# Relu-squared attention and a GELU layer pair: one more batch of the first layer as seven half-size products, in a new order of operations

## The chip, the cores and the metric

The kernel runs on one core of a Trainium2 chip. The metric is the device time of one run, in microseconds (us), given as the median of some runs. The engines have the short names of the profile: PE is TensorE (matrix products), PEld its weight loads, DVE is VectorE, ACT is ScalarE, POOL is GpSimd, SP is SyncE. A "q" behind a name (SPq, POOLq) is the engine's own queue of instructions, among them the issues of DMA transfers.

## The reference

Attention with relu squared in place of softmax goes straight into a two-layer perceptron with exact GELU. There are 8 batches, 12 heads, 448 positions and head size 64; the perceptron sees 3584 rows of 768 columns and has 2048 hidden columns. Inputs and output are float32.

```python
scores = (q @ k.transpose(0, 1, 3, 2)) / sqrt(64)       # 8 x 12 x 448 x 448
attn = maximum(scores, 0) ** 2 / 448
attn_out = attn @ v                                     # 8 x 12 x 448 x 64
x = attn_out.transpose(0, 2, 1, 3).reshape(3584, 768)
h = x @ w_in                                            # 3584 x 2048
g = 0.5 * h * (1 + erf(h / sqrt(2)))
out = g @ w_out                                         # 3584 x 768
```

## The kernel before

**Attention.** The work goes by batch (0 to 7) and, in a batch, by three groups of four heads. One step (`add_steps`) makes the scores of one 128-row block of K for all 448 columns of Q: two products each into the two halves of a PSUM tile `ps`, on quarters of PE's array (64 x 64, L736). ACT or DVE then takes relu into `a_sq` (L748, L750), and DVE squares it in place (L757). After seven steps of a group `add_av` multiplies by V (L797, also 64 x 64) into `pav`, and two copies put the result into `xT`, the transposed input of the perceptron. `QK2.1` below means the scores of batch 2, group 1.

**Where Q and K come from.** POOL issues the loads of Q, K, V and of both weight matrices, which also turn float32 into bf16. Q and K must be transposed. Batches 0 and 1 do so on PE (`add_tk`, `add_tq`). Batches 2 to 7 use DMA transposes issued by SP (`add_T_dma`, L662): nine for each batch, three per group, which are K, the even slots of Q and the odd slots of Q. The odd slots of a group also need the Q load of the next group. POOL keeps its loads apart from transposes by gates: `add_gate(b, g)` (L703) is a small copy of what group g's transposes have written, so that POOL, and all that it has to issue after that, waits until these have landed. `qT` and `kT`, the tiles that transposes write, exist twice, and so the transposes of batch b wait for the scores of batch b - 2.

**The first layer** reads `xT` of a batch. In the plain form (`add_f1`, L849) it is 16 column blocks of six products with 448 moving columns, with the result in `psh`; ACT applies GELU into `h_sb` (L859). In block form (`add_blocks`, `add_block`, L993) the layer is cut as a 2 x 2 block matrix (halves of the 768 inputs, of the 448 rows, and of the 2048 outputs), and a scheme with seven half-size products in place of eight is used. Its sums of weights (`add_wsums`) are made once on DVE; for each batch DVE also makes four sums of x halves (`xsum`, tile `xs`), and combines the products in passes (`passed`, L1030, tile `part`), from which ACT takes GELU (L1039). Before the change batches 5, 6 and 7 have this form; their weight sums overwrite part of `w_in`, so the last plain first layer must be over.

**The second layer** runs over 14 groups of 256 rows (`add_group`), each again by seven products (L1166) of 8 x 384 columns. DVE makes sums of `h_sb` (L1147) and combines the products into two tiles `osb` of 128 rows (L1200), which SP stores (`store_rows`, L1127). There are three `osb` buffers; each group takes two, and a buffer is free when its store has landed. The last product of the last group is cut in two, of `LAST` and 384 - `LAST` columns. The rows of group 0 are done plainly (`add_plain`).

**The order.** All of these are operations given to a `Scheduler`, which numbers them as they are added. The order in which each engine issues its operations is written out in a string, `ORDER`. A word is an engine (P for PE, A for ACT, D for DVE, G for POOL, S for SP) and an operation's number; `Z` and a number stands for a filler on PE (`add_fill`), products with zeros of so many columns, that are used for nothing. Every engine issues strictly in the order of its words; an operation that is not ready holds all behind it on its engine. What waits on what follows from the data and the tile buffers.

Of the kernel before, what the change touches and what calls it, by code (L numbers as in the profile page):

```python
# [26 lines left out]
KF = FF // 128  # L27
# [24 lines left out]
LEAD = 8  # L52
HALF_M = 6
# [30 lines left out]
G0 G1 G2 G3 G1435 G4 G5 G6 A10 P11 D13 A16 P17 G7 D12 P14 D18 P42 P39 G8 P19 A15 P21 D43 P33 P36 D44  # L84
A40 D20 Z128 A22 P54 G9 P25 P23 A37 D34 P51 D26 P48 A55 Z1056 D35 A24 P69 D56 Z1024 D41 A49
P57 Z992 D38 A52 P63 Z448 G117 D70 P45 A58 D53 P66 A64 D50 P27 A46 G118 P31 D59 P60 D28 A67
G119 D32 A47 P78 P29 D65 G120 A61 P81 Z1088 D68 D30 A79 P93 D62 P108 Z544 D71 A82 P84 Z992
G121 A94 P75 D109 P72 G122 D83 A85 P90 P129 D80 G123 D73 A76 P105 A74 P102 D95 G124 P131 D130
A91 P141 D86 A106 D77 P111 P96 D132 A103 P165 P143 D92 A112 D104 D107 A97 P156 D113 P87 G125
D98 A166 P99 D110 G126 D88 A157 P114 A142 D100 A89 P174 G127 A101 P168 D115 P133 A144 P135  # L90
A116 G128 D175 P171 P159 A169 D134 P251 D136 D170 A160 P145 D158 A172 D167 A252 P162 P186 D176
P192 P243 A146 D161 G147 D173 A187 G148 P253 D193 A163 A244 D164 P195 G149 P180 P198 P137 A254
G150 P139 D196 A181 P183 P177 G151 D138 A199 D140 A184 P189 P219 P245 D178 G152 A190 D185 P247
G153 D194 A220 D179 A246 G154 P213 D188 P222 P204 P263 D221 A248 G155 D197 A214 D200 P265 D191
A205 D182 A264 P261 A223 A266 P216 D224 S231 P207 P201 D206 A262 A208 S229 P210 P259 D209 A217
D215 S232 P255 D211 A260 P249 D212 D218 A256 D202 P225 A203 S228 A250 P257 S230 A226 P267 D227
A258 P348 S234 A268 P350 S233 A349 P352 G237 A351 G238 P354 S235 A353 G239 P288 S236 P294 P282
P358 A355 G240 G241 D289 P356 D283 A359 P360 D295 A357 D290 P306 P279 P276 D296 P362 A361 D307
P364 D280 A363 P366 D277 A365 P368 A367 P370 A369 P300 P285 P291 G242 P372 A371 G269 D286 A292
P374 G270 D284 A373 G271 P318 P303 D301 P312 G272 P376 D308 A375 G273 A304 D319 P378 D278 A377  # L100
P380 D313 A379 D293 G274 D314 D390 P382 D305 G275 D302 A381 D391 D287 D281 P330 P309 P297 S398
D392 A331 D320 P315 S399 P384 D393 A298 D396 A310 S401 A383 D417 P387 D394 D419 A385 D311 A299
D395 A316 D317 P324 P321 D418 A325 P333 D397 P327 A388 P421 D420 D322 S400 A328 D323 P423 D326
A334 D422 S386 P339 P336 P342 P425 D424 D329 A343 D335 P427 S402 A426 D337 P429 G407 A340 G408
S403 D428 P431 G409 D344 D338 S389 D341 P440 P437 D332 P345 S404 D430 A438 P443 D441 P446 S405
P433 D432 A346 D347 A444 P509 A447 D434 P511 D439 G410 D448 S406 A510 G411 P449 D442 P452 G412
P455 P513 D562 A512 S435 D445 S436 A453 P515 D454 A450 A514 P517 D456 D451 P464 D457 P461 P458
S541 A465 P467 D462 A518 P470 G413 S542 P519 A516 G414 A459 G415 P521 D471 S543 G416 D472 A520
P523 D466 A468 D460 S544 A522 P479 D560 P476 P473 D469 P525 A524 D463 A477 P527 D480 A474 D478
A526 P529 D475 D481 A528 P488 P485 P482 S545 A489 P494 D486 A530 P491 P531 D487 D483 P533 D495  # L110
A532 S546 P535 D496 A484 D561 A492 P503 D490 P500 A534 P497 D493 P537 A536 G550 G551 S547 P564
D498 G552 A538 D504 S548 P539 D499 A501 G553 A565 D505 P600 G554 D502 P603 P506 G555 S549 A601
P606 D604 A540 P609 P566 D563 A507 D602 P568 D607 D567 P570 D610 A569 A508 P572 D571 P624 P612
P618 S704 P574 D580 D608 A613 D573 P576 S705 G556 A619 D581 G557 D582 P627 S706 D575 P615 G558
P584 D614 G559 D577 S578 A616 D611 P586 S707 D605 A628 D617 A625 P636 D620 P630 S579 A585 P621
D629 G713 A631 D637 P633 G714 P588 D587 S708 G715 A622 D626 D623 A634 P639 P642 P648 D583 P590
D638 A640 D635 A589 D632 P592 D641 A643 D591 P651 A649 S709 D644 P657 P645 D593 A652 P666 D658
P654 P594 D653 A646 D659 A655 D650 P596 A647 D667 S710 D595 P660 P766 P663 P672 D597 A661 D767
P674 A664 S711 D662 A673 D656 P676 D668 A675 D665 P772 P769 P669 S712 G716 D773 A770 P763 S598
P775 A677 G717 P678 S599 D670 G718 A764 D771 P680 G719 D723 A776 S867 D768 A679 P790 P778 D765  # L120
A671 P781 G720 P682 A681 D777 G721 D791 P684 G722 S868 D725 A683 P686 D779 A782 A685 P688 D783
D780 D774 P787 P793 P784 D724 S869 A788 P799 D794 A687 P796 P690 A689 D795 D789 A797 P692 D798
A691 P694 A693 P696 A785 A695 S870 P698 A786 A800 P802 P811 A697 P805 D801 P700 A699 A803 D812
P702 S871 D792 A806 D804 P814 P817 D807 P808 A815 S872 P823 D818 A701 P820 P727 G876 D816 A703
G877 D809 S873 A821 G878 D726 P729 A810 D819 A728 D822 P826 D813 A824 P829 S874 P906 P731 D730
G879 A830 G880 D827 S875 P733 G881 A907 D828 D831 P912 D825 P921 P832 D745 A913 P909 A732 D922
P924 P735 D734 A833 A925 P737 A910 D743 A834 P936 D914 P918 P933 D736 P739 D738 S741 D744 A934
P747 D908 G882 A937 D740 G883 P749 D938 A919 S978 G884 D935 A748 G885 D926 P942 P930 S742 P915
P751 D750 A931 D943 S979 P753 D920 A916 A752 D746 P755 D923 S980 D911 D944 P948 P945 D917 P927
D888 A949 D754 P939 P757 D950 A928 D886 D756 P759 A946 D887 A940 D758 A929 P835 D932 D947 D941  # L130
S981 P957 P954 P951 A836 D958 A955 P960 P963 D760 P837 D959 A961 D952 P839 D956 A953 S982 A838
P966 D964 P972 P969 D962 P841 A840 S983 D889 A973 D965 P843 S984 A842 D967 P847 A970 S985 A844
P845 D971 D968 S761 D974 P990 P987 D1067 P975 S986 A991 P993 D988 A846 P996 S762 P849 D992
A848 D1068 A976 D1070 P851 A997 D989 A850 P853 A994 A977 D995 P1005 P1002 A852 P999 P855 A854
D1006 A1003 P859 D1004 A1000 D998 A856 P857 D1007 D1001 P1011 P1014 P1008 D1059 A858 A1012
P1017 D1015 P1026 P861 A1009 D1063 A860 P863 D1060 A1018 D1010 P1020 A1027 P1029 D1061 P1023
A862 P865 D1016 A864 D1019 P890 A1021 D1028 D1022 A866 P892 D1062 A1024 A891 D1013 P894 D1025
A1030 D1069 D893 P1035 D1031 P1038 P1032 D1064 A895 A1036 D1066 P1041 D1037 A1039 P1044 P896
D1033 A1042 D1034 D1040 P898 A1045 D1043 D897 P1047 D1046 P1050 P1053 P900 D899 A1048 D1139
P902 D1049 A1051 D1140 A1054 P1071 D1052 D1055 P1056 D901 S904 A1072 D903 S905 P1088 D1141  # L140
P1073 D1057 P1090 A1089 D1058 P1143 D1074 D1091 P1075 D1065 P1092 A1144 P1077 D1142 A1076
D1179 P1094 A1093 D1180 P1079 D1078 P1096 D1095 P1145 D1080 D1097 A1081 P1082 D1181 A1098
P1099 D1146 P1085 D1083 P1102 D1100 A1084 P1105 D1086 A1101 P1122 D1103 A1087 P1107 D1182
A1106 P1124 A1123 P1147 A1104 D1108 D1125 P1109 P1126 A1148 P1111 A1110 P1128 A1127 P1113
D1112 P1130 D1129 P1149 D1114 D1131 A1115 P1116 A1132 P1133 D1150 P1119 D1117 P1136 D1134
A1118 P1151 D1120 A1135 D1137 A1121 P1153 D1291 A1138 D1292 D1152 P1155 D1159 D1154 S1157
P1163 D1160 D1156 S1158 P1165 D1161 D1164 P1167 D1162 D1166 D1293 P1169 D1294 A1168 P1171
D1170 P1173 D1253 D1172 P1175 D1251 D1174 S1177 P1183 D1252 P1200 D1176 S1178 P1185 A1184
D1254 P1202 A1201 P1255 D1186 D1203 P1187 P1204 A1256 P1189 A1188 P1206 A1205 P1191 D1190
P1208 D1207 P1257 D1192 D1209 A1193 P1194 A1210 P1211 D1258 P1197 D1195 P1214 D1212 A1196  # L150
P1217 D1198 A1213 P1234 D1215 A1199 P1219 A1218 P1236 A1235 P1259 A1216 D1220 D1237 P1221
P1238 A1260 P1223 A1222 P1240 A1239 P1225 D1224 P1242 D1241 P1261 D1226 D1243 A1227 P1228
A1244 P1245 D1262 P1231 D1229 P1248 D1246 A1230 P1263 D1232 A1247 D1249 A1233 P1265 A1250
D1264 P1267 D1271 D1266 S1269 P1275 D1272 D1268 S1270 P1277 D1273 D1276 P1279 D1274 D1278
P1281 D1280 P1283 D1282 P1285 D1365 D1284 P1287 D1363 D1286 S1289 P1295 D1364 P1312 D1288
S1290 P1297 A1296 D1366 P1314 A1313 P1367 D1298 D1315 P1299 P1316 A1368 P1301 A1300 P1318
# [240 lines left out]
def kernel(  # L397
# [537 lines left out]
    def add_blocks(b):  # L935
# [34 lines left out]
        for m4 in (0, M1 // 2):  # L970
# [4 lines left out]
            for p in zip(*todo):  # L975
                atoms += [(0.58, o) for o in p]
# [445 lines left out]
    def at(b, n):  # L1422
        return [at_slot(b, n)]
# [112 lines left out]
```

## Time and profile before

| | us |
|---|---|
| three runs | 369.36, 370.3, 371.55 |
| median | 370.3 |
| span of the profiled execution | 367.9 |
| PE busy | 359.3 (98%) |
| DVE busy | 285.1 (78%) |
| ACT busy | 199.4 (54%) |
| POOL busy | 62.9 (17%) |
| granted clock of PE, mean share of full speed | 0.997 |

The span is that of one execution taken by the profiler, from its first instruction to its last. The profiled execution's own device time is not recorded beside it; its span lies 2.4 below the median of the three runs and 1.5 below the fastest of them. Busy times are sums of instruction durations, and PE's is over 3573 products.

### The profile page before, as it was taken

Reading aid. Unit: us, or ns where it says so; the run is one execution under the profiler, and the core shown is the slowest. Engines: PE = TensorE matmul, PEld = TensorE weight load, DVE = VectorE, ACT = ScalarE, POOL = GpSimd, SP = SyncE. Lnnn points to the kernel's source line nnn. Section 1 sums busy time; section 2 is a strip of 40 time slices with the busy share of each in tenths; the row PEclk is TensorE's granted clock in tenths of the full one; section 3 lists DMA queues with packets and bytes.
Section 4 is the critical chain, followed back from the end, with each engine's and each line's share of the span. In section 5 each row is a group of like instructions: output and inputs, shape, how many; then the busy total and the mean of one; then the engine's idle time right before and its main releaser. Section 6 shows DMA issues by size and latency. Waiting matters only on the chain.

```text
span 367.9 us, 8474 instructions
## 1 busy us (share of the span) xinstructions
PE 359.3 (98%) x3573; PEld 222.5 (60%) x3573; DVE 285.1 (78%) x473; ACT 199.4 (54%) x319; POOL 62.9 (17%) x103
## 2 busy tenths in 40 slices
PE   7999999999999999999999999999999999999995
PEld 6675654455544455544555544557876897688663
DVE  4998854699788889989598997998788558665862
ACT  5998954536367546765777568863540353045200
POOL 8766304230112140240302000000000000000000
PEclk9999999999999999999999999999999999999998
DMA  9999999999999999999999980002002301210233
GB/s 180 191 202 204 201 178 167 196 201 178 162 218 214 154 186 193 237 214 154 166 110 131 215 183 2 2 2 86 3 0 87 88 0 52 86 37 2 86 87 86
DMA packets 89542, 47.27 MB, mean 128 GB/s; under 512 B 55329, under 2 KB 86049, under 8 KB 89505
## 3 DMA queue, kind: packets, MB, share of 16 engines
q0 software_dynamic: 32912, 22.47, 43.8%
q1 hardware_dynamic: 55952, 23.76, 34.9%
q8 instruction: 28, 0.46, 0.5%
q10 hardware_dynamic: 640, 0.51, 0.4%
q14 instruction: 10, 0.07, 0.1%
HBM read 45.61 MB, written 11.01 MB: 154 GB/s over the span
## 4 chain that ended last, share of the span: by engine, by line
PE 78%; DMA 8%; SPq 5%; DVE 5%; issue 1%; POOL 1%; ACT 1%; DVEq 0%; POOLq 0%; ACTq 0%
PE pso L1166 30%; PE psh L849 19%; PE pb L993 13%; PE ps L736 8%; PE pav L797 7%; SPq L662 5%; DMA wout_sb<-in_moe_w_out_dram 4%; DVE a_sq L757 2%; DMA nq<-in_q_dram 1%; DVE t_sb L1103 1%; DMA qT<-nq 1%; DMA out_dram<-osb 1%; ACT a_sq L748 1%; PE tp L635 1%; DVE part L1030 1%
## 5 line engine op out<-in xcount | busy, mean ns | idle before, releaser
L748 ACT ACTIVATE a_sq<-ps 128x896 bf16<-128x896 f32 (+1 forms) x119 | 104.3, 918 | 36.8 <-PE ps L736 36.6
L757 DVE TENSOR_TENSOR a_sq<-a_sq 128x896 bf16<-128x896 bf16 (+1 forms) x169 | 97.0, 617 | 9.4 <-ACT a_sq L748 8.8
L849 PE MATMUL psh<-xT,win_sb 128*128 128x448 bf16 (+1 forms) x516 | 96.4, 340 | 0.4 <-issue 0.4
L849 PEld LDWEIGHTS <-win_sb 128*128 128x128 bf16 x516 | 48.1, 98 | 45.8 <-issue 9.7
L750 DVE TENSOR_SCALAR a_sq<-ps 128x896 bf16<-128x896 f32 (+1 forms) x50 | 53.5, 1078 | 17.1 <-PE ps L736 17.0
L859 ACT ACTIVATE h_sb<-psh 128x448 bf16<-128x448 f32 x80 | 43.2, 548 | 29.9 <-PE psh L849 29.6
L1166 PEld LDWEIGHTS <-s_sb 128*128 128x128 bf16 x424 | 40.7, 98 | 26.6 <-issue 2.0
L1030 DVE TENSOR_TENSOR part<-pb,part 128x448 f32<-128x448 f32 x60 | 34.6, 620 | 21.5 <-PE pb L993 21.5
L736 PE MATMUL ps<-qT,kT 64*64 64x448 bf16 (+1 forms) x756 | 47.9, 336 | 0.5 <-ACT a_sq L748 0.2
L1166 PEld LDWEIGHTS <-h_sb 128*128 128x128 bf16 x312 | 29.6, 98 | 22.5 <-issue 4.4
L1166 PE MATMUL pso<-wout_sb,s_sb 128*128 128x384 bf16 (+2 forms) x216 | 38.1, 320 | 0.1
L1166 PE MATMUL pso<-wout_sb,h_sb 128*128 128x384 bf16 x208 | 38.1, 326 | 0.0
L1166 PE MATMUL pso<-t_sb,s_sb 128*128 128x384 bf16 x208 | 38.1, 326 | 0.0
L797 PE MATMUL pav<-a_sq,v_sb 64*64 64x448 bf16 (+1 forms) x756 | 36.5, 329 | 0.3 <-issue 0.2
L736 PEld LDWEIGHTS <-kT 64*64 64x64 bf16 x756 | 18.5, 105 | 22.9 <-issue 17.1
L1039 ACT ACTIVATE h_sb<-part 128x448 bf16<-128x448 f32 x36 | 20.1, 578 | 20.2 <-DVE part L1030 19.9
L1200 DVE TENSOR_TENSOR osb<-pso,p_sb 128x384 f32<-128x384 f32 x39 | 21.7, 556 | 11.0 <-PE pso L1166 6.7
L993 PEld LDWEIGHTS <-win_sb 128*128 128x128 bf16 x288 | 27.6, 98 | 2.3 <-issue 0.4
L797 PEld LDWEIGHTS <-v_sb 64*64 64x64 bf16 x756 | 21.2, 107 | 11.7 <-issue 1.3
L703 POOL COPY gate<-qT 128x16 bf16<-128x16 bf16 x15 | 3.7, 246 | 111.0 <-DMA qT<-nq 111.0
L993 PEld LDWEIGHTS <-ws 128*128 128x128 bf16 x216 | 20.7, 98 | 0.0
L1147 DVE TENSOR_TENSOR s_sb<-h_sb 128x1024 bf16<-128x1024 bf16 x26 | 17.8, 685 | 2.3 <-PE pso L1166 2.3
(61 smaller groups left out, 298.4 us busy)
## 6 DMA issues: line engine op xcount, KB each, us to landing
nk<-in_k_dram POOLq DMA_DIRECT2D x23, 224.0 KB, 5.6
nq<-in_q_dram POOLq DMA_DIRECT2D x21, 224.0 KB, 8.3
v_sb<-in_v_dram POOLq DMA_DIRECT2D x5, 672.0 KB, 13.9
out_dram<-osb SPq DMA_DIRECT2D x8, 336.0 KB, 2.9
v_sb<-in_v_dram POOLq DMA_DIRECT2D x9, 224.0 KB, 8.6
out_dram<-osb SPq DMA_DIRECT2D x7, 288.0 KB, 3.2
out_dram<-osb SPq DMA_DIRECT2D x8, 240.0 KB, 3.0
win_sb<-in_moe_w_in_dram POOLq DMA_DIRECT2D x8, 192.0 KB, 8.6
```

The source lines that it names most:

```text
L736: nc.tensor.matmul(ps[64 * j : 64 * j + 64, e, x * w : x * w + w], kT[r, g, i * 128 + 64 * j : i * 128 + 64 * j + 64], moving, start=True, ...
L748: A.activation(ar, ps, AF.Relu, scale=c_att)
L750: V.tensor_scalar(ar, ps, c_att, 0.0, op0=mybir.AluOpType.mult, op1=mybir.AluOpType.max,)
L757: V.tensor_mul(box["a2"][:, :, :used], ar, ar)
L797: nc.tensor.matmul(pav[0][o2 : o2 + 64, e, :w], vt[b][r, 2 * g + e, bass.ts(i, D)], box["a2"][r, y, o : o + w], start=(i == 0), stop=(i == ...
L849: nc.tensor.matmul(ph[:, x * n : x * n + n], win_sb[:, kd, bass.ts(m + x, 128)], xT[b][:, kd, c], start=(kd == 0), stop=(kd == KD - 1),)
L859: A.activation(h_ring()[:, m : m + nm, o + c.start : o + c.stop], box[0][:, :S].rearrange("p (x n) -> p x n", x=nm), AF.Gelu,)
L993: nc.tensor.matmul(bank[name][:, y, z * HS : z * HS + HS], w[:, k, bass.ts(mm, 128)], right()[:, k], start=first and k == 0 and z == 0, st ...
L1030: V.tensor_add(get(to), ps(name), get(other))
L1039: A.activation(h_ring()[:, m : m + 2, o + half[c].start : o + half[c].stop], src().rearrange("p (x n) -> p x n", x=2), AF.Gelu,)
L1166: nc.tensor.matmul(box[bank][:, n0:n1], left()[:, kf], right()[:, kf, n0:n1], start=bool(need) and kf == 0, stop=kf == K2 - 1, skip_group_ ...
L1200: V.tensor_add(out()[:, n0:n1], box[bank][:, n0:n1], other()[:, n0:n1])
```

## The change

Batch 4's first layer, plain before, is made in block form (`NBLK = 4`, where three batches had it). The weight sums are therefore made after the first layer of batch 3, and the sums `xs` of batch 6 and not 7 take a `qT` buffer, while batch 7's wait for the first products of batch 4's blocks (`first_blocks`). In the list of work, the first layer of batch 4 leaves batch 5's attention and comes behind the attention of batch 7, where the end part begins (`end`). Group 6 of the second layer is added one batch earlier.

The whole `ORDER` is another one. Up to number 762 the same numbers mean the same operations in both.

```diff
+NBLK = 4
...
 ORDER = """
...
-A40 D20 Z128 A22 P54 G9 P25 P23 A37 D34 P51 D26 P48 A55 Z1056 D35 A24 P69 D56 Z1024 D41 A49
-P57 Z992 D38 A52 P63 Z448 G117 D70 P45 A58 D53 P66 A64 D50 P27 A46 G118 P31 D59 P60 D28 A67
-G119 D32 A47 P78 P29 D65 G120 A61 P81 Z1088 D68 D30 A79 P93 D62 P108 Z544 D71 A82 P84 Z992
...
+P25 A40 D24 P36 G118 D44 P19 A34 D26 P66 G9 P21 D41 A37 P69 D20 Z640 D22 P48 A67 P57 D35 P29 A70
...
-D215 S232 P255 D211 A260 P249 D212 D218 A256 D202 P225 A203 S228 A250 P257 S230 A226 P267 D227
-A258 P348 S234 A268 P350 S233 A349 P352 G237 A351 G238 P354 S235 A353 G239 P288 S236 P294 P282
-P358 A355 G240 G241 D289 P356 D283 A359 P360 D295 A357 D290 P306 P279 P276 D296 P362 A361 D307
...
+P225 A202 G237 S235 G269 A203 P276 P285 P259 D226 S236 A277 A227 P279 D286 P291 P288 S234 P354
+A280 A260 D289 P294 S231 P282 P362 A292 D290 A355 G242 S232 G149 P366 D283 A295 D278 G238 A363
+P327 G239 P324 P342 A367 P350 A325 G240 G272 P374 D343 G241 D281 A351 D284 P303 P336 D296 P358
...
-P1419 D1418 S1424 P1420 D1421 S1425 D1422 S1426
+S1421 P1427 D1424 S1218 D1420 P1429 D1425 D1428 P1431 D1426 D1430 P1433 D1432 P1435 D1434 P1437
+D1436 P1439 D1443 D1445 D1438 P1447 D1444 D1440 S1442 P1449 S1422 D1448 S1441 P1451 D1450 P1453
+D1452 S1463 P1455 D1446 D1454 P1457 D1456 P1460 P1459 D1458 S1464 D1462 D1461 S1465 S1466
 """
...
 # add_blocks
+    first_blocks = []
...
-                    tag = "qT" if b == B - 1 else "kT"
+                    tag = "qT" if b == B - 2 else "kT"
...
-        gone = [o for (bb, *_), o in QK.items() if bb == (B - 2 if b == B - 3 else B - 1)]
+        gone = [o for (bb, *_), o in QK.items() if bb == (B - 2 if b == B - NBLK else B - 1)]
+        if b == B - 1:
+            gone += first_blocks
...
             for p in zip(*todo):
                 atoms += [(0.58, o) for o in p]
+                if b == B - NBLK:
+                    first_blocks.extend(p)
...
-    F1B = {2: 1, 3: 2, 4: 3, 5: 4}
-    GROUPS = {2: (1,), 3: (2, 3), 4: (4, 5), 5: (6,)}
+    F1B = {2: 1, 3: 2, 4: 3}
+    GROUPS = {2: (1,), 3: (2, 3), 4: (4, 5, 6)}
...
-    add_wsums(at(B - 1, 1), [F1[B - 4, m, None] for m in range(KF)])
+    add_wsums(at(B - 1, 1), [F1[B - NBLK - 1, m, None] for m in range(KF)])
...
-    end = woven(add_blocks(B - 3), add_group(7))
+    end = add_blocks(B - 4)
+    end += woven(add_blocks(B - 3), add_group(7))
```

What the words of the three stretches mean:

- Fills. Before has eight, Z128, Z1056, Z1024, Z992, Z448, Z1088, Z544 and Z992, all in the first third of batch 0 and 1's attention; after has one, Z640.
- Transposes and loads of batches 2 and 3. S228 to S236 are batch 2's nine transposes, three for each group in order (K, even Q, odd Q). G237, G240 and G242 are the gates on its groups 0, 1 and 2; G149, G152 and G155 load V of batch 2, G238, G239 and G241 load `w_out`, G269 to G274 load K and Q of batch 3, and G275 loads V of batch 3 whole. Before, POOL issues G149, G152 and G155 between the K and Q loads of batch 2, then G237 G238 G239 G240 G241 G242 and the loads of batch 3. After, it issues the K and Q loads of batch 2 first, then G237 G269 G242 G149 G238 G239 G240 G272 G241 and the rest, and SP issues the transposes S229 S228 S230 S233 S235 S236 S234 S231 S232. S231 and S232 are group 1's K and even Q, and go last. Group 1's first scores (P303, P306, P300 begin them) are put behind group 0's (P276 first). For batch 3, SP issues S398 to S406 with S405, group 2's odd Q, last, behind G410, G407 (gates 3.1 and 3.0) and G275; G413 (gate 3.2) waits for it.
- The second layer's stores. In the list of after, S1217 and S1218 store group 8, S1309 and S1310 group 9, S1329 and S1330 group 10, S1421 and S1422 group 11, S1441 and S1442 group 12; the first number of a pair is rows 128 to 255, the second rows 0 to 127. Before, SP has every pair in the order of the groups. After, S1218 stands behind S1421 and S1422 behind S1442. Elsewhere, the stores of the second layer's first groups (S386 and S389 are group 0's two halves, S435 and S436 group 1's) stand among transposes in both lists, in after further back: S386 behind all nine of batch 3's transposes, where before it stands between the fourth and the fifth.

- The last product of group 13. Before, its 256 columns (P1419) come ahead of its 128 (P1420); after, the 128 (P1460) come ahead of the 256 (P1459).

All that is between these stretches stands in another order too. Counted over the whole list, relus on DVE are 56 in after and 50 in before, and PE goes from quarter-array to full-array work or back 124 times in after and 109 times in before.

## Prediction

> **What bounds the kernel now.** I read the page first, its busy times and its chain by engine.
>
> ```profile
> PE 359.3 (98%) x3573; PEld 222.5 (60%) x3573; DVE 285.1 (78%) x473; ACT 199.4 (54%) x319; POOL 62.9 (17%) x103
> ...
> PE 78%; DMA 8%; SPq 5%; DVE 5%; issue 1%; POOL 1%; ACT 1%; DVEq 0%; POOLq 0%; ACTq 0%
> ```
>
> PE is busy for 98% of the span and carries 78% of the chain. Time leaves only if PE gets less work or waits less, and every wait that the new order puts before PE is paid in full. The rest of the chain is the transposes' queue (SPq), DMA and DVE: what PE waits for when it waits. Second, busy times by stage:
>
> ```profile
> 5.00:32.00 27.00, 24.68 (x561) 17.57 (x562) 24.39 (x48) 24.34 (x38) 18.66 (x27) 1.00 1.36 197
> ...
> 100.00:250.00 150.00, 149.69 (x1427) 77.17 (x1424) 130.92 (x209) 100.02 (x152) 21.70 (x37) 1.00 0.98 147
> 250.00:364.00 114.00, 113.29 (x928) 87.26 (x926) 79.50 (x142) 34.73 (x67) 0.00 (x0) 1.00 0.17 52
> ```
>
> The columns after the length are PE, weight loads, DVE, ACT and POOL, the granted clock, the DMA share and GB/s. Before 32 us PE, DVE and ACT are all near 24.5 of 27. From 100 us PE is full, DVE has 87%, and DMA works almost until attention ends. Third, the chain in order of time, for what PE work costs:
>
> ```profile
> 107.60 3.51 PE psh L849 x18
> ...
> 163.38 2.38 PE psh L849 x12
> ...
> 166.44 4.65 PE psh L849 x24
> ...
> 254.71 3.45 PE pb L993 x36
> ...
> 259.46 4.60 PE pb L993 x48
> ```
>
> Twelve more first-layer products (x12 to x24) cost 4.65 - 2.38 = 2.27, so one of 448 columns is 0.189. Eighteen are then 3.40, yet 3.51 stands there: each stretch pays 0.11 for the change between quarter-array work (scores, A@V, transposes) and full-array work. Twelve more block products cost 1.15, so one of 224 columns is 0.0958. Fourth, the timeline at PE's largest gap after the start-up:
>
> ```profile
> 94.68 1.00 SPq L1127 DMA_DIRECT2D out_dram<-osb  x2
> ...
> 97.39 1.46 PE L1166 MATMUL pso<-t_sb,s_sb 128*128 128x384 bf16 x8
> ...
> 98.64 0.56 DVE L1200 TENSOR_TENSOR osb<-pso,p_sb 128x384 f32<-128x384 f32 x1 [1.82 <-DMA out_dram<-osb]
> ...
> 99.25 1.46 PE L1166 MATMUL pso<-t_sb,h_sb 128*128 128x384 bf16 x8 [0.40 <-DVE osb L1200]
> ```
>
> A store stood behind transposes in SP's queue, so its osb buffer came free late; the eviction waited 1.82 and the next product of the same bank started at 99.25 instead of 97.39 + 8 x 0.1625 = 98.69.
>
> **The change, part by part** (us; the sum is on this execution's span, 367.9, which lies 2.4 below the runs' median 370.3; I add it to the median).
>
> Block form for batch 4. Gone are 96 products of 448 columns, 96 x 0.189 = 18.16. New are 7 products x 8 column blocks x 3 = 168 of 224 columns, 168 x 0.0958 = 16.10: **-2.06**. DVE gets 20 more additions (L1030, 0.62 busy each), 4 more xsums (0.50) and, by the list, 6 more relus (1.09): 21 us more work. It lies beside PE, but the layer also leaves attention, so the same relus and squares must be done in some 18 us less (131 of 150 becomes about 131 of 132 by busy times; three squares in a row take 1.69 in the chain, 0.56 each and not 0.62, so 119 of 132). Bounds 0 and 1.5 (about the 1.74 for which the chain at 241 us goes through ACT's relu); I take **+0.5**, nearer to none.
>
> Fills. The eight fills have 6272 columns, the one left has 640: 5632 x 0.189/448 = 2.38. They stood on waits for relus, and DVE and ACT are as full there as PE, so from 0 (waits laid bare) to -2.38. The new list puts other work there (a transpose and two products of batch 1 and scores that stood later), so **-2.0**.
>
> Changes of array mode, counted in the two lists: 109 before, 124 after: 15 x 0.11 = **+1.65**.
>
> Waits that go: at 98.69 (0.56) and again at 102.36 (eight scores took 0.87, elsewhere 0.57): **-0.9**, since the list now puts the first store after all nine transposes and group 1 later. At 242.5 and 273.6 PE waits 0.35 and 0.23 on ACT and DVE; other neighbours now: **-0.6**, at worst 0.
>
> Transposes of batch 2. The first scores of batch 2 have 47.06 us of PE work and 32 mode changes ahead before, 39.04 and 41 after (the operations ahead of them in each list, at the trace's mean duration for each kind). So they come 8.02 - 0.99 = 7.0 earlier than 60.0, at 53, and group 1's at 62.6. Three V loads (1.15 each) move behind the K and Q loads, so the last of these lands at about 48 instead of 50.15. Transposes then land some 1.3 apart, the last two, group 1's K and even Q, at 59.4 to 60.7. But POOL's gate on group 2 no longer waits for these two: behind it POOL issues V of group 0 and the wout loads. What that does the trace shows, by issues (x, KB if given, us to landing):
>
> ```profile
> qT<-nq SPq DMA_TRANSPOSE x1, 3.3
> ...
> qT<-nq SPq DMA_TRANSPOSE x1, 10.9
> ```
>
> The first went at 57.2 with no load running, the second at 59.87 beside the wout load. If caught, 57.5 + 7 to 11 lands at 64.5 to 68.5, 2 to 5.9 too late; if not, 0. I take **+2.2**, between the ends, as the margin between last transpose and first load is under 1 us. The scores queue in PE's order with all that follows, so nothing fills it.
>
> Transposes of batch 3. The last (group 2's odd Q) is issued behind the gate whose next load is V of batch 3, one load of 1.38 MB. A transpose beside such a V load took 12.4 at 112.85, alone 3.0 to 4.4. PE wants it at about 100.5, issue is about 92: 0 to 4 late, **+1.2**.
>
> Later batches. Their transposes now run after their loads rather than interleaved, and have 2 to 6 us before their first use where they had 10 to 25. Price 0 to 3, held in the range.
>
> Stores in the second layer. The list sends the store of group 8's first row (S1218) behind group 11's, and group 11's (S1422) behind group 12's first: one of the three osb buffers is held, and groups 10 and 13 must wait for the store of the group before. Worked out: last product of group 12 ends, eviction 0.8, second part of the store issued 0.5 later, landing 2.9 (SP's L1127 median), addition 0.6, together 4.8; PE has three products, 3 x 1.30 = 3.9. So 0.9 twice, **+1.8**; it is 0.8 if stores land in 2.4, and 2.4 if in 3.2.
>
> Tail. The last second-layer piece has 256 columns, not 128: addition 425 ns instead of 281, a larger last store: **+0.2**.
>
> Sum: -2.06 + 0.5 - 2.0 + 1.65 - 0.9 - 0.6 + 2.2 + 1.2 + 1.8 + 0.2 = **+2.0**, so 372.3.
>
> The Trainium skill's "Advanced Engine Details and Errata", X-Bar Transpose (TRN2), says that transpose DMAs are as fast as regular ones. The trace agrees for lone ones (3.3) and not beside loads (10.9, 12.4). By the rule both transposes' terms would be 0 and the sum -1.4.
>
> Against the fills' removal speaks the skill's "TensorE: Matmul & The Clock Gate", Part 1: an idle window of about 3.4 us halves PE's clock. The rows show 1.00 throughout with gaps of at most 1.1, and I expect none longer before 60 us; by the rule a cold window there would cost about 3.4 more.
>
> **Rivals.** *All transposes land in time (the other side).* One mechanism: the two last transposes of batch 2 have left the DMA queues before the first V or wout packet. Point: group 1's even Q lands by 62.6. For it: gate, issue and start of a load need some 2 us after group 2's landing, two transposes 2.6 less the landing's own delay. Against it: landings in this trace slip by 1 to 2 us even alone (3.0 to 4.4). Then 2.2, 1.2 and 0.5 fall away: -1.9, 368.4; with the fills' whole 2.38 and quick stores, 367.
>
> *One of the waits shows, the others do not.* Without the batch 2 wait -0.2, without the batch 3 wait and DVE's +0.3: 370 to 371.5, no difference that counts.
>
> *The lateness feeds itself.* Caught transposes hold POOL's next gate, so the next batch's loads and transposes come late too, and the 2 to 6 us before first use are gone at each batch. That adds two or three waits of 1 to 1.5: 375 to 377. For it: POOL waits 111.0 us at its gates already. Against it: K and Q loads no longer run between transposes.
>
> That the block form is not what it says can be left out: the list has the 168 products and no first-layer product of batch 4.
>
> **How the numbers follow.** Forecast with the self-feeding case on its slow side: 0.58 for slower. One wait alone: 0.28. In time: 0.14. What a measurement of this kernel can tell from no change is about 0.5%, 1.85 us; 372.3 is past it by a little, the rival at 368.4 just past it on the other side. Low end 368.6 (the in-time case's likely value), high 376.5 (batch 2 caught by 5 and one later wait); below and above I leave about 1 in 10 each.
>
> **What would show it.** Block form: 96 fewer psh products, 168 more pb at 0.096. Transposes: a gap of PE before scores (L736) at 62 to 65 us released by a DMA into qT, and one near 101. Stores: DVE's L1200 waiting on out_dram twice after 320 us. Wrong if PE's gaps between 55 and 105 sum to under 1 us, or if POOL's loads after group 2's gate start after the last batch 2 transpose.

## The result, and the profile after

The changed kernel takes 386.84 us in the median of four runs (385.02 to 390.25), before takes 370.28 beside it: a ratio of 1.046, 95% interval 1.0405 to 1.0515. Forecast were 372.3 and a range up to 376.5: the direction was right, the size was not. The profiled execution is the longest of the four (390.25, span 388.5), so its waits sum to some us more than the median's. Some executions of any kernel here take over 1.5% longer than its fastest; the medians and ratios below leave these out.

The page of after, PE, the chain by engine, and the group of the scores (busy and mean ns of one, then the idle time ahead of it and what ended it):

```profile
PE 361.4 (93%) x3631; PEld 229.7 (59%) x3631; DVE 303.2 (78%) x505; ACT 192.1 (49%) x315; POOL 64.0 (16%) x103
...
PE 45%; DMA 27%; SPq 16%; issue 4%; DVE 4%; POOL 3%; ACT 0%; DVEq 0%; POOLq 0%
...
L737 PE MATMUL ps<-qT,kT 64*64 64x448 bf16 (+1 forms) x756 | 49.8, 342 | 14.9 <-DMA qT<-nq 13.2
```

PE had 98% and is at 93%; its part of the chain fell from 78% to 45%, and DMA with SP's queue of transposes now carry 43%. The scores wait 14.9 us where the page of before has 0.5. PE's waits as the trace sums them (us in total, times, longest):

```profile
PE ps L737 <- DMA qT<-nq: 13.2, 5, 4.9
PE pso L1173 <- DVE osb L1207: 4.5, 3, 2.0
```

By stage (columns as in the prediction: length, PE, weight loads, DVE, ACT, POOL, granted clock, DMA share, GB/s), PE is no longer full anywhere from 100 us to the end of attention, and it is not DVE that is full in its place:

```profile
100.00:150.00 50.00, 44.39 (x416) 21.21 (x409) 40.17 (x62) 29.69 (x46) 10.40 (x17) 0.97 1.17 163
150.00:200.00 50.00, 45.02 (x446) 22.74 (x444) 43.86 (x71) 28.67 (x43) 11.37 (x20) 1.00 1.16 177
200.00:250.00 50.00, 45.88 (x464) 26.91 (x463) 40.56 (x68) 29.12 (x43) 1.25 (x2) 0.97 0.63 102
```

What is full is the row of the DMA engines, tenths of busy time in 40 slices of the span (9 is 90% or more). First the page of before (a slice is 9.2 us), then that of after (9.7 us):

```profile
DMA  9999999999999999999999980002002301210233
```

```profile
DMA  9999999999999999999999941000020022022233
```

In both the digit is 9 for the first 23 slices, up to the end of attention's transfers: 211 us in before, 223 in after. The digit says that packets were under way, not that no more bytes could have moved: in these slices GB/s goes from 110 to 237 in before and from 133 to 203 in after. The prediction had this in front of it and read only "DMA works almost until attention ends". The last scores start at 246.5 us in before and at 245.6 in after, though by the prediction's durations of products after has 23 us less PE work ahead of them (18.2 of it batch 4's layer). From there to PE's last product it is 116.9 us in before and 138.5 in after. So the work was moved, and the place that it left was not closed up.

### The profile page after: what moved, and what is told of

It reads as the page before. It is cut to its first block, busy times and chain, and to the rows that moved or that the text cites. A ratio compares the mean times of both kernels' runs of the same rounds, so it can differ in the third digit from the quotient of the medians.

```text
span 388.5 us, 8622 instructions
## 1 busy us (share of the span) xinstructions
PE 361.4 (93%) x3631; PEld 229.7 (59%) x3631; DVE 303.2 (78%) x505; ACT 192.1 (49%) x315; POOL 64.0 (16%) x103
## 4 chain that ended last, share of the span: by engine, by line
PE 45%; DMA 27%; SPq 16%; issue 4%; DVE 4%; POOL 3%; ACT 0%; DVEq 0%; POOLq 0%
PE pso L1173 20%; PE pb L1000 16%; SPq L663 15%; DMA nq<-in_q_dram 15%; DMA qT<-nq 7%; PE pav L798 3%; DMA nk<-in_k_dram 3%; PE ps L737 3%; PE psh L850 3%; DMA out_dram<-osb 2%; DVE a_sq L758 1%; DVE osb L1207 1%; SPq L1134 1%; POOL gate L704 1%; POOL wout_sb L493 1%
## 5 line engine op out<-in xcount | busy, mean ns | idle before, releaser
L749 ACT ACTIVATE a_sq<-ps 128x896 bf16<-128x896 f32 (+1 forms) x113 | 100.4, 923 | 57.4 <-PE ps L737 57.3
L850 PE MATMUL psh<-xT,win_sb 128*128 128x448 bf16 (+1 forms) x420 | 78.1, 337 | 0.3 <-issue 0.3
L751 DVE TENSOR_SCALAR a_sq<-ps 128x896 bf16<-128x896 f32 (+1 forms) x56 | 60.0, 1079 | 17.3 <-PE ps L737 16.7
L737 PE MATMUL ps<-qT,kT 64*64 64x448 bf16 (+1 forms) x756 | 49.8, 342 | 14.9 <-DMA qT<-nq 13.2
L1037 DVE TENSOR_TENSOR part<-pb,part 128x448 f32<-128x448 f32 x80 | 46.7, 619 | 14.8 <-PE pb L1000 13.1
L860 ACT ACTIVATE h_sb<-psh 128x448 bf16<-128x448 f32 x64 | 34.8, 550 | 24.9 <-PE psh L850 24.8
L1046 ACT ACTIVATE h_sb<-part 128x448 bf16<-128x448 f32 x48 | 24.7, 573 | 12.4 <-DVE part L1037 10.3
L1000 PEld LDWEIGHTS <-ws 128*128 128x128 bf16 x288 | 27.7, 98 | 1.7
L704 POOL COPY gate<-qT 128x16 bf16<-128x16 bf16 x15 | 5.1, 339 | 111.8 <-DMA qT<-nq 104.9
L1000 PE MATMUL pb<-xT,win_sb 128*128 128x224 bf16 x192 | 22.2, 259 | 0.0
## 6 DMA issues: line engine op xcount, KB each, us to landing
nk<-in_k_dram POOLq DMA_DIRECT2D x23, 224.0 KB, 10.2
```

Source lines behind the costliest of these rows:

```text
L737: nc.tensor.matmul(ps[64 * j : 64 * j + 64, e, x * w : x * w + w], kT[r, g, i * 128 + 64 * j : i * 128 + 64 * j + 64], moving, start=True, ...
L749: A.activation(ar, ps, AF.Relu, scale=c_att)
L751: V.tensor_scalar(ar, ps, c_att, 0.0, op0=mybir.AluOpType.mult, op1=mybir.AluOpType.max,)
L850: nc.tensor.matmul(ph[:, x * n : x * n + n], win_sb[:, kd, bass.ts(m + x, 128)], xT[b][:, kd, c], start=(kd == 0), stop=(kd == KD - 1),)
L860: A.activation(h_ring()[:, m : m + nm, o + c.start : o + c.stop], box[0][:, :S].rearrange("p (x n) -> p x n", x=nm), AF.Gelu,)
L1000: nc.tensor.matmul(bank[name][:, y, z * HS : z * HS + HS], w[:, k, bass.ts(mm, 128)], right()[:, k], start=first and k == 0 and z == 0, st ...
```

## The experiments

Two theories. **A:** attention can't end earlier, since the transport of Q, K and V (loads, DMA transposes, gates) has a pace of its own, which PE's work only just covered; what leaves attention leaves a hole and is paid again at the end. **B:** the transport has room, and the new order of loads and transposes on POOL and SP made it late. Each kernel was measured beside before on its own chip (369.97, 370.12 and 370.22 in the three sets).

**1. Before, with batch 4's layer cut in place.** The order is untouched.

```diff
-                for kd in range(KD):
+                for kd in range(KD - 1 if b == 4 else 0, KD):
...
-                        start=(kd == 0),
+                        start=(kd == (KD - 1 if b == 4 else 0)),
```

> The kernel before, order untouched, with batch 4's plain first layer cut from 96 products to 16 (only the last of each six is made; the rest of the layer's inputs are left out). 80 x 0.189 = 15.1 us of PE work leave the attention stage. Theory A, the transport of Q, K and V (loads, transposes, gates) sets the length of attention and PE's work hardly covered it: the last scores of batch 7 stay near 246 us, PE waits for qT instead, and the time stays at 365 to 370. Theory B, the transport had room in this order and only the new order of queues made it late: the work leaves the path, 355 to 357.

Measured: 366.81, ratio 0.9919 (0.9900 to 0.9939). Of 15.1 us only 3.2 came back, A's number, but not by A's resource. The stages where batch 4's layer stands, in this kernel:

```profile
205.00:215.00 10.00, 8.94 (x113) 4.45 (x104) 9.98 (x18) 7.82 (x12) 0.00 (x0) 1.00 1.16 197
215.00:225.00 10.00, 6.26 (x65) 2.29 (x63) 8.82 (x15) 8.70 (x16) 0.00 (x0) 1.00 0.68 137
225.00:235.00 10.00, 8.44 (x69) 3.42 (x69) 9.27 (x14) 7.31 (x13) 0.00 (x0) 0.66 0.01 2
```

and in before:

```profile
215.00:225.00 10.00, 10.00 (x95) 4.99 (x94) 8.01 (x14) 7.24 (x12) 0.00 (x0) 1.00 0.45 108
```

PE has holes, and DVE is at 8.8 to 10.0 of 10. No wait of PE is for the transport: of 5.9 us between 205 and 240 us, 4.0 are for the GELUs on ACT of the cut layer itself and 1.9 for relus on ACT and DVE. This run keeps the layer's 16 GELUs, which the change takes out of attention, so it overstates the bound; experiment 5 is without them. The run points to a second resource just behind PE there; it doesn't decide between A and B for the transport.

**2. After, with three quarters of the K and Q loads left out (batches 3 to 7).** Of Q one head of four is loaded, of K half the partitions of one row of two; the rest of the tiles keeps older data.

```diff
+        if b > 2:
+            g1 = g0 + 0.25
...
+            if b > 2:
+                nc.gpsimd.dma_start(nk[b][:64, 2 * g0 : 2 * g0 + 1], kv_view(k, b, g0, g1)[:64, :1])
```

> The kernel after with the K and Q loads of batches 3 to 7 cut to a quarter of their bytes (one head of four for Q; 64 of 128 partitions and one of two rows for K; the rest of those tiles keeps older data). Transposes, V loads, gates and the order stay. Both theories expect PE's 13.6 us of waits for qT and kT to go, since either a shorter transport or earlier loads heal them: 371 to 375, with the waits for osb (4.5 us) left. If PE's waits stay although three quarters of the loads' bytes are gone, the transposes and gates alone set the pace, and neither theory has the right resource: 382 to 388.

Measured: 369.69, ratio 0.9993 (0.9979 to 1.0007), 17.2 less than after and level with before. The largest of PE's waits that are left:

```profile
PE pso L1180 <- DVE osb L1214: 2.9, 2, 1.6
PE tp L643 <- DVE a_sq L765: 1.0, 1, 1.0
```

None of the scores' waits is for qT or kT, and PE is full again, as in the last stage of attention:

```profile
200.00:250.00 50.00, 50.00 (x512) 35.63 (x511) 48.31 (x86) 28.47 (x46) 0.00 (x0) 1.00 0.11 33
```

DVE has 48.3 of 50 there and does not hold PE up, so DVE is not what lengthens after. The whole loss beyond the stores hangs on the transport. It came out lower than expected (371 to 375) since the third wait for osb (2.0 at 168 us, where a store stands among transposes) and the slowed clock after long waits went too.

**3. The same cut in before,** as the control.

> The kernel before with the same cut of the K and Q loads of batches 3 to 7 to a quarter. PE waits there for transport only behind osb (0.56 at 98.7 us) and 0.30 at 102.4 us, so both theories expect 368.5 to 370. The difference to the same cut in after is the two orders' difference without the transport: by PE's work and its mode changes (-4.4 + 1.65) after should be 0 to 3 us faster by itself, before the osb waits (4.5).

Measured: 369.18, ratio 0.9977 (0.9968 to 0.9987): 0.8 us, as expected. The transport cost before nothing that matters, and after 17.

**4. The two late stores of after moved forward** (SP's words alone).

```diff
-S1198 S1310 S1309 S1329 S1330 S1421 S1218 S1442 S1422 S1441
+S1198 S1218 S1310 S1309 S1329 S1330 S1421 S1422 S1442 S1441
```

> The kernel after with two words of SP's order moved: the store of group 8's first row stands right behind group 7's stores, and that of group 11's first row right behind the other half of group 11. Nothing else changes. Both theories: the waits of groups 10 and 13 for an osb buffer (1.43 and 1.41 us beyond the products' own time) go, -2.8, 383.5 to 384.5. If the wait only moves to the next group, under 1 us is gained.

Measured: 383.33, ratio 1.0381 (1.0324 to 1.0438) to before, 3.5 less than after (by medians on two chips, 2.9 by the ratios; experiment 8 has the same step at 3.25). The waits of groups 10 and 13 are gone from the trace; one for osb is left, at 170 us, where a store still stands behind transposes:

```profile
PE pso L1173 <- DVE osb L1207: 3.1, 1, 3.1
```

**5. The block form alone, in the order of before.** Batch 4's layer is taken out of attention and its blocks are put as one stretch ahead of batch 5's (PE's words alone; the sums and passes go with them, and the numbers are those of each kernel).

```diff
-P835 P837 P839 P841 P843 P847 P845 P849 P851 P853 P855 P859 P857 P861 P863 P865
+P1039 P1056 P1041 P1058 P1043 P1060 P1045 P1062 P1047 P1064 P1050 P1067 P1053 P1070
+P1073 P1090 P1075 P1092 P1077 P1094 P1079 P1096 P1081 P1098 P1084 P1101 P1087 P1104
```

> The block form for batch 4 alone: the order of before on every engine, without batch 4's plain first layer, its blocks put as one stretch behind attention and ahead of batch 5's (the pattern of batch 5's blocks; 8 fills kept). Theory A, whatever the order, attention can't become shorter by the 18 us that leave it (the cut layer of the run before gave back only 3.2 of 15.1 us): about 366.8 - 0.6 (the last sixth, hidden in the same share) + 16.1 (blocks) + 0 to 3 (their passes, with no other products woven in) = 380 to 386. Theory B, the new order loses the time and the block form is worth its 2.06 us: 368 to 372.

Measured: 388.9, ratio 1.0486 (1.0436 to 1.0535): not told from after, whose interval overlaps, and far from B's 368 to 372. Its waits and its worst stage:

```profile
PE ps L738 <- ACT a_sq L750: 4.3, 7, 1.0
PE pav L799 <- DVE a_sq L759: 3.7, 4, 2.4
```

```profile
225.00:235.00 10.00, 8.80 (x64) 3.89 (x64) 10.00 (x16) 5.36 (x7) 0.00 (x0) 0.50 0.01 2
```

It has A's number again and not A's resource: no wait here is for qT. The hole is where the layer was taken out, and there DVE is full, now without the layer's GELUs. PE's clock falls to 0.50 in it, which may be why the size came out 3 us above the 380 to 386 expected; no run separates that. So no order of these two makes the block form of this batch pay.

**6. After, with the five V loads of batches 3 to 7 left out** (these batches use batch 2's V).

```diff
+            if b > 2:
+                vt[b] = vt[2]
+                return
             get_v(b)
```

> The kernel after with the five V loads of batches 3 to 7 left out (1.38 MB each; these batches use batch 2's V). Nothing of the chain K and Q load, transpose, gate is changed. If what bounds is how much the DMA engines move (A, by volume): 5 loads x 3.5 us of the engines' time leave, and most of the 13.2 us of waits go, 371 to 376. If it is the chain of one batch's K and Q after the other's through a single nq and nk buffer (A, by the chain), V only runs beside it: 381 to 386.

Measured: 371.21, ratio 1.0027 (0.9996 to 1.0058), 15.6 less than after, though no K, Q, transpose or gate was touched. What is left of the scores' waits:

```profile
PE ps L740 <- DMA qT<-nq: 1.8, 1, 1.8
```

So not only the bytes of the chain through `nq` and `nk` count. But this run doesn't show that volume alone decides. The V loads stand in POOL's queue between the gates, and the four slowest transposes of after (14.27, 13.75, 11.90 and 11.50 us) all run beside one. Without them batch 7's last transpose lands 25 us earlier, 5 us for each load, where the engines' time alone was put at 3.5. Bytes and lengthened transposes left together.

**7. After, with 45 us of PE work taken out** (the plain layers of batches 1, 2 and 3 cut as in experiment 1).

> The kernel after with the plain first layers of batches 1, 2 and 3 cut from 96 products to 16 each (only the last of each six is made): 45 us of PE work leave the stretch from 56 to 206 us, and the transport is as in after. Theory A by volume: the transport has a pace of its own, batch 7's last transposes land at 212 to 223 us as before (222.9 in after), PE waits for qT 40 us and more, the time falls by under 12. If the transport only followed PE (transposes waiting for scores of two batches before, loads for transposes), they land before 195, and the time falls by 30 or more.

Measured (one run): 385.56, 1.3 less than after's median. The page and the scores' wait:

```profile
PE 337.8 (88%) x3391; PEld 213.4 (56%) x3391; DVE 302.0 (79%) x505; ACT 190.3 (50%) x315; POOL 64.1 (17%) x103
```

```profile
PE ps L737 <- DMA qT<-nq: 13.4, 6, 3.8
```

The wait for qT did not grow to the 40 us expected of A, since the rest of the room went into waits for relus, squares and GELUs on ACT and DVE (7.1 + 4.4 + 2.0 + 1.7 + 1.3 + 1.0 = 17.5 us by the same list; the 7.1 are for GELUs of plain layers, which this cut leaves in place) and into products at a lower clock (0.94 over the run). But in this order of the queues the transport has its own pace, as A says. When the last of a batch's nine transposes lands, read from the trace's transposes (us):

| | batch 3 | 4 | 5 | 6 | 7 |
|---|---|---|---|---|---|
| before | 111.2 | 135.2 | 159.9 | 192.4 | 218.8 |
| after | 107.5 | 132.3 | 161.6 | 197.6 | 222.9 |
| after, 45 us less PE work (7) | 107.0 | 133.1 | 158.1 | 194.2 | 219.2 |
| after, K and Q loads to a quarter (2) | 100.2 | 118.5 | 142.0 | 172.1 | 195.7 |
| after, no V loads (6) | 101.3 | 125.8 | 149.1 | 175.5 | 197.9 |
| after, old order of the queues (9) | 109.2 | 128.4 | 160.6 | 185.5 | 210.1 |
| the same with the stores forward (9) | 110.2 | 131.4 | 164.1 | 195.2 | 215.3 |

With 45 us less to do PE pulls the end of the transport forward by 3.6 us; fewer loads do it by 25 to 27. The last transposes of after land at most 5.2 us later than those of before (batch 6), and those of batches 3 and 4 earlier. PE is there earlier.

**8. After with both: quarter loads and stores forward.**

> The kernel after with both edits of the earlier runs: K and Q loads of batches 3 to 7 cut to a quarter (the rest of the tiles keeps older data), and the two stores S1218 and S1422 moved forward. Theory A: nothing of PE's waits is left but the start-up, 369.7 - 2.9 = 366.5 to 367.5, about 0.6% under the same cut in before (369.2): the new plan for PE is worth that much when the transport doesn't bind. If the stores' wait moves on to the next groups, as it did in part before (3.1 at one place), 368 to 369.5.

Measured: 366.44, ratio 0.9895 (0.9871 to 0.9920). Against the same cut in before (369.18) the new plan for PE is worth 2.7 us, once the transport no longer binds it.

**9. After with the old order of transposes and loads, without and with the stores forward.** SP's transposes of batches 3 to 7 by groups; POOL from batch 3's V load on:

```diff
-G410 G407 G275 G413 G409 G415 G412 G408 G414 G411
+G275 G407 G408 G409 G410 G411 G412 G413 G414 G415 G416
...
```

> The kernel after with the old order on POOL's and SP's queues from batch 3's V load on: gate on group g of a batch, then the next batch's K and Q of group g, V last, and the transposes by groups. Stores stay in the places between transposes that after gives them; PE, ACT and DVE keep the order of after. Theory B, long blocks of loads and of transposes are what makes them late: the waits of PE for qT (13.2 us) go for the most part, 372 to 378. Theory A, the transport's total sets the pace: 383 to 392, since PE's order was made for the other one.

> The kernel after with the old order of transposes and loads from batch 3 on, and with the two stores moved forward: 383.2 - 3.5 = 379.7 if the two gains add up, and that is what an order of queues alone can give back of 16.5 us: theory A says that it stays above 376, theory B that 372 can be reached.

Measured: 383.16, ratio 1.0312 (1.0257 to 1.0368), and 376.84, ratio 1.0184 (1.0133 to 1.0235). The order of the queues gives back 3.7 us alone and 6.5 with the stores (383.33 to 376.84), or 5.5 and 7.3 by the ratios, of the 17 that hang on the transport. B holds for that part, and the table has the reason: the same bytes end at 210.1 (in the fastest of four runs) and 215.3 us instead of 222.9, so the pace in A is not fixed either, it depends on the order. The second kernel still has

```profile
PE ps L737 <- DMA qT<-nq: 7.6, 3, 4.9
```

**10. Before with one store earlier** (`S386` ahead of `S400`), the one small wait of before that the forecast counted as gone.

> The kernel before with one word of SP's order moved: the first store of the second layer (S386) ahead of the transpose S400 that SP waits for until 91.8 us, instead of behind it (the store is ready at 87.4 us, it is issued at 94.7). All theories: PE's wait at 98.7 us (0.56) goes, 0.1 to 0.2% faster, 369.3 to 369.9 beside 370.0; it can't be more than 0.9 (with the 0.30 at 102.4).

Measured: 369.58 beside 370.12, ratio 0.9984 (0.9961 to 1.0007). The wait for osb is gone from the trace, the gain is not told from none. No version here that does the whole work beats before by more than can be measured: the plan of after for PE reached 366.44, but only with three quarters of the K and Q loads left out.

## Why the prediction was wrong, and where it was right

**The step that failed** is the reading of what bounds the kernel. It was "Time leaves only if PE gets less work or waits less", and for the 18 us that leave attention it asked DVE alone (+0.5). It never asked when the transfers as a whole would be done, though the DMA row was full until 210 us. The transport was then priced as single late transposes: +2.2 for batch 2, +1.2 for batch 3, "0 to 3, held in the range" for the later batches. In the runs these three terms together are 17.15 (386.84 - 369.69), less 1.1 that before itself has (370.28 - 369.18; 0.8 beside before on the same chip): 16.0 where 3.4 stood in the sum. The direction came out right in part by luck: without the +2.2, which did not happen, the forecast's sum stands at -0.2.

- Batch 2's +2.2 was wrong as such: its scores began at 54.0 (53 forecast), the last two transposes landed at 60.7 and 61.7, and no gap stands at 62 to 65. V's load was issued at 59.95, after the last transpose (58.52), and that one took 3.17; here the rival "all land in time" was right, and one of the prediction's signs of being wrong came true.
- Batch 3's last transpose was caught as described: issued at 98.34 beside a V load issued at 97.81, it took 9.16 and landed at 107.5. PE waited 4.94, where 0 to 4 was the bound and 1.2 was taken; the batch's first scores had already waited 1.35, until 93.7.
- Batches 4 to 7 lost more: PE stands 0.47 us ahead of scores until 129.9, 0.45 until 152.3, 2.35 until 197.7 and 4.12 until 216.5, together 7.4, where "0 to 3" was the bound for all. With batch 3's 6.3 that is 13.7 in the profiled execution. By the same trace, experiment 2 also takes away 3.4 us lost to a lower clock after the two longest waits and a wait of 2.0 for a store that stood among transposes: 19.1 in this longest of the four runs, where the medians differ by 17.15.
- The rival "the lateness feeds itself" had the place, the sign and a link that the chain of after shows: a transpose lands late beside a load, the gate behind it holds POOL, and the next loads and transposes come from there.

```profile
98.34 9.16 DMA qT<-nq
107.67 0.53 issue
108.20 3.98 DMA nq<-in_q_dram
112.31 1.82 SPq L663
...
184.83 0.49 POOL v_sb L567
...
187.08 12.45 DMA nq<-in_q_dram
199.67 1.25 SPq L663
...
212.20 4.22 DMA qT<-nq
216.50 0.57 PE ps L737 x8
```

From 42.5 to 216.5 us this chain holds no product at all; in before the chain runs on PE from 102.85 on. The rival's price, 375 to 377, was too low: it added two or three waits of 1 to 1.5 us, and the trace has six, up to 4.94. The transfers hardly came later than in before, where transposes beside V loads took as long (12.36 at 112.85 us). PE came earlier, and at most batches waits anew for a stream that ends near 220 us in this order of the queues. Such a stream is to be priced as a whole: the work taken from before its end (23 us) less what other work fills. How the 16.0 divide between what no order avoids (A) and the new order itself (B) stays open; experiment 9 puts B at 4 to 7.

**The stores** went as worked out, in place and kind: DVE's additions of groups 10 and 13 waited for `out_dram` (2.64 at the first), PE twice. They cost 3.3 to 3.5 and not 1.8: the two stores landed in 3.50 and 3.07 where 2.9 was taken, and PE lost 1.43 and 1.42 at the two places, not 0.9. What else is in the 3.3 no run shows.

**The sum of the terms on PE was right.** Block form, fills, array mode, DVE, small waits and tail sum to -2.06 - 2.0 + 1.65 + 0.5 - 0.6 + 0.2 = -2.3 (without the 0.9 that the cut in before also loses); experiments 3 and 8 show -2.7. No run shows one of these terms by itself, so errors may cancel. One is doubtful: by the traces PE changes between quarter-array and full-array work 93 times in before and 99 in after if its transposes count as quarter-array work, as the prediction has them; 108 and 124 come out if they count as full. By its own definition the term is 6 x 0.11 = 0.66 and not 1.65. DVE's "119 of 132" doesn't come out either: the trace has 108 squares in that stretch, so 0.06 less for each is 6.5 and not 12. And the range's low end stands at 368.6, while the rival that it is taken from adds up to 368.4.

The 16.56 measured splits by these differences into -2.7 for PE's plan, +3.3 for the two stores and +16.0 for the transport (medians of four chips, on which before differs by 0.3).

On the rules that were weighed: alone, with no load under way, transposes took 3.1 to 4.6 in after, beside loads up to 14.3. The prediction set such numbers against the sentence of the Trainium skill's "Advanced Engine Details and Errata", X-Bar Transpose (TRN2), that transpose DMAs are as fast as regular ones. But regular loads are slow there too: in after the K loads of 224 KB took a median of 10.2, and the V load beside the transpose of 9.16 took 9.4. So these runs don't contradict the sentence; it gives no price for sharing, and to read it as a price of 0 would have put the sum on the wrong side. The cold window that was priced at 3.4 costs less here: 1.7 after each of the two longest waits (worked out in the last section).

## What to carry to other kernels

When work is taken away from the busiest engine in a stage, list what else is busy in that stage to the end, the DMA row included, and ask of each when it would be done if the engine were infinitely fast; the earliest end that the stage can have is the latest of these. For queues that hold each other up, follow the loop (here load, transpose, gate, next load) and not the single transfer. With a second resource near 90% in the same stretch the gain can end after a few us, as here, and work put off to a later stage is then paid there in full. Two cheap runs show this beforehand: cut the engine's work in place and see whether the end moves, and cut the other resource's volume and see whether the engine's waits go.

## What the runs showed of the hardware

A wait of PE costs more than its length. After the wait of 4.94 us in after, one second-layer product (eight instructions) took 2.74 us; those around it took 1.47 and 1.48. The timeline, and the windows behind it with the granted clock as third column from the end:

```profile
101.22 1.48 PE L1173 MATMUL pso<-t_sb,s_sb 128*128 128x384 bf16 x8
107.64 0.38 PE L737 MATMUL ps<-qT,kT 64*64 64x448 bf16 x4 [4.94 <-DMA qT<-nq]
107.96 2.74 PE L1173 MATMUL pso<-wout_sb,s_sb 128*128 128x384 bf16 x8
...
111.68 1.47 PE L1173 MATMUL pso<-t_sb,h_sb 128*128 128x384 bf16 x8
```

```profile
107.00:110.00 3.00, 2.36 (x11) 1.18 (x12) 0.00 (x0) 0.92 (x1) 2.00 (x4) 0.66 0.37 109
110.00:113.00 3.00, 3.00 (x24) 1.18 (x23) 2.26 (x5) 1.39 (x2) 2.44 (x4) 0.77 1.24 156
113.00:116.00 3.00, 3.00 (x45) 1.72 (x47) 2.97 (x6) 2.06 (x3) 0.00 (x0) 1.00 1.07 148
```

The Trainium skill's "TensorE: Matmul & The Clock Gate", Part 1, says that the clock is at half after at least one idle window of about 3.4 us. This wait agrees, and so does the one of 4.12 us at 216.5 (0.53 and 0.90 in the two stretches of 3 us from 217); after the wait of 2.35 at 197.7 the clock stayed at 1.00. Experiment 1 goes further: the clock was at 0.50 from 226 to 232 us though none of PE's gaps in the 20 us before was over 1.7 us. PE had been busy for 1.31, 2.61, 1.84 and 1.15 us in the four stretches of 3 us before it. Many short gaps can cost the clock too. In after the lost clock is 3 x (0.34 + 0.23) = 1.7 us at the first place and 3 x (0.47 + 0.10) = 1.7 at the second, 3.4 in all, a part of the 16 that no row of waits shows. (The means over the whole execution, 0.990 in after and 0.997 in before, also count the time behind PE's last product.)
